# Attention and two feed-forward layers on one core: earlier norms, a shorter weight conversion, and engine order written out in the source

## The chip, the cores and the metric

The kernel runs on one core of a Trainium2 chip. Its time is the device time of one execution in microseconds (us); a smaller number is better. Five things run side by side and wait for each other by semaphores: TensorE (PE, matrix products into PSUM), VectorE (DVE), ScalarE (ACT), GpSimd (POOL), and the DMA engines, to which SyncE (SP) hands transfers. SBUF is the working memory.

## The reference

The input is q, k and v of 6016 rows (tokens) and 256 columns, all float32.

```python
qn = q / (np.linalg.norm(q, axis=1, keepdims=True) + 1e-06)   # columns scaled, over the 6016 rows
kn = k / (np.linalg.norm(k, axis=1, keepdims=True) + 1e-06)
s = kn.transpose(0, 2, 1) @ qn / tau                          # 256 x 256
a = np.exp(s - s.max(-1, keepdims=True)); a /= a.sum(-1, keepdims=True) + 1e-09
x = v @ a                                                     # 6016 x 256
h = x @ w_in                                                  # 256 -> 2048
P = a[0] + a[1] * h + a[2] * h**2 + a[3] * h**3
Q = 1.0 + np.abs(b[0]) * np.abs(h) + np.abs(b[1]) * h**2
y = (P / (Q + 1e-06)) @ w_out                                 # 2048 -> 256
h = y @ w_in2
out = (h * np.clip(h + 3.0, 0.0, 6.0) / 6.0) @ w_out2         # 6016 x 256
```

## The kernel before

**Opening: q and k.** q and k come in 14 chunks of up to 4 rows per partition (QK_CHUNKS, loop at line 173). Each chunk is multiplied into k^T q in PSUM (`sp`, line 196), squared on ACT (line 189) and added up on DVE (line 191) for the norms. Between chunks, four groups of the first input weights are loaded (`wi1`, W_IN_AT, line 177) and converted (`conv`). After the last chunk TensorE sums the squares over the partitions (line 215), DVE and ACT make the norms (lines 217 to 228), and a softmax of two halves follows (lines 232 to 249). Its transpose `eT` times `wi1` gives the fused weight `w1` (`emit_w1`, line 253), so that the first layer reads v directly.

**Weight conversion.** A float32 weight arrives as two words per number, and `conv` (line 102) rebuilds it as a float32 `f` from a low word L and a high word H: two ACT operations (lines 110 and 111), a DVE shift-and-or (line 112), and a second DVE operation for the sign bit (lines 116 and 119). Then `f` is split into a high part (ACT, line 123) and a rest (GpSimd, in two groups DVE, line 125). There are 16 groups: 4 each of `wi1`, `wo1`, `wi2`, `wo2`.

**The steps.** The 6016 tokens are one block of 384 and eleven of 512; each block has 8 steps for layer one, each step 256 of the 2048 columns. Step s runs, for different blocks at once: M1 (first product, line 281) into `h`; U1, U2, DS for the denominator, P1, P2, P3 for the numerator, LN and EX (the reciprocal as exp(-ln)); one step later HI, N2, DD, LO, which form the quotient as a high part and a rest; M3 (line 286), two steps later, into `y`. The second layer follows 10 steps behind: M2, C1, C2, H2, L2, and M4. Each of M1 to M4 is 12 matmuls. The end of a block adds Y (splitting y), O (the output) and V (splitting the next v). In steps below 20, DS is on GpSimd (line 338), below 16 LO too (line 459); L2 goes to GpSimd from step 17 on (line 393). `M1@4` below means M1 of step 4.

**What sets the order.** Each step is emitted by a list of names (ORDERS, one of three by step), with weight conversions at W; a scheduler then orders each engine's instructions by the time at which it expects them to be ready. Buffers are few (BUFS); `h` has two PSUM tiles in the first 10 steps and one afterwards. DMAs are issued by SP in the order of the source.

Of the kernel before, what the change touches and what calls it, by code (L numbers as in the profile page):

```python
# [41 lines left out]

@with_exitstack
def attention_rational_relu6_kernel(ctx: ExitStack, tc, q, k, vT, tau, w_in, w_out, ca, cb, w_in2, w_out2, outT):
# [128 lines left out]
    for i, n in enumerate(QK_CHUNKS):  # L173
# [3 lines left out]
        if i in W_IN_AT:  # L177
# [351 lines left out]
```

## Time and profile before

| | |
|---|---|
| median of 3 runs | 1174.41 us (1174.01 to 1175.34) |
| profiled execution | 1176.72 us, of which the span of the trace is 1175.0 us |
| busy share of the span | PE 95%, DVE 88%, ACT 70%, POOL 27% |
| mean granted TensorE clock | 0.976 of full speed |

The page divides the span into 40 slices and gives each engine's busy share in them. A busy PE is not a PE at its peak: at half its clock it is as busy as at the full one. So the granted clock stands beside the busy time, and the idle time of an engine counts only where it is the one that others wait for.

### The profile page before, as it was taken

Reading aid. Unit: us, or ns where it says so; the run is one execution under the profiler, and the core shown is the slowest. Engines: PE = TensorE matmul, PEld = TensorE weight load, DVE = VectorE, ACT = ScalarE, POOL = GpSimd, SP = SyncE. Lnnn points to the kernel's source line nnn. Section 1 sums busy time; section 2 is a strip of 40 time slices with the busy share of each in tenths; the row PEclk is TensorE's granted clock in tenths of the full one; section 3 lists DMA queues with packets and bytes.
Section 4 is the critical chain, followed back from the end, with each engine's and each line's share of the span. In section 5 each row is a group of like instructions: output and inputs, shape, how many; then the busy total and the mean of one; then the engine's idle time right before and its main releaser. Section 6 shows DMA issues by size and latency. Waiting matters only on the chain.

```text
span 1175.0 us, 12284 instructions
## 1 busy us (share of the span) xinstructions
PE 1110.8 (95%) x4858; PEld 915.3 (78%) x4858; DVE 1035.5 (88%) x861; ACT 822.3 (70%) x801; POOL 315.0 (27%) x136
## 2 busy tenths in 40 slices
PE   7866778899999999999999999999999999999998
PEld 6735666678888888888888888888888888888886
DVE  6699999999998998998998998998998998999943
ACT  6687786577767767777776776777777677776543
POOL 0027667633221222122122122222212212222200
PEclk9978989899999999999999999999999999999999
DMA  9952000001001001001001001001000000000000
GB/s 360 383 189 92 18 1 1 1 1 32 1 1 36 1 1 36 1 1 36 1 1 37 1 1 36 1 1 37 1 7 30 1 18 19 1 19 1 1 18 18
DMA packets 17450, 42.21 MB, mean 36 GB/s; under 512 B 1520, under 2 KB 2544, under 8 KB 17392
## 3 DMA queue, kind: packets, MB, share of 16 engines
q1 hardware_dynamic: 17392, 41.43, 9.7%
q8 instruction: 38, 0.62, 0.2%
q14 instruction: 20, 0.16, 0.0%
HBM read 35.26 MB, written 6.16 MB: 35 GB/s over the span
## 4 chain that ended last, share of the span: by engine, by line
PE 79%; DVE 6%; issue 4%; DMA 4%; POOL 3%; ACT 2%; SPq 1%; POOLq 0%; DVEq 0%; ACTq 0%
PE h L281 40%; PE o L286 20%; PE y L286 19%; DMA lo<-in_q_dram 2%; POOL B L338 1%; POOL lo L459 1%; DVE B L446 1%; DMA U<-in_k_dram 1%; DVE hi L440 1%; DVE P L452 1%; DMA raw_wo<-in_moe_w_out_dram 1%; DVE q L119 1%; DVE q L112 1%; DVE P L346 1%; DVE P L351 1%
## 5 line engine op out<-in xcount | busy, mean ns | idle before, releaser
L393 POOL TENSOR_TENSOR lo<-C,hi 128x1024 fp32r<-128x1024 f32 (+1 forms) x80 | 191.9, 2399 | 665.2 <-DVE lo L461 567.7
L281 PE MATMUL h<-vh,w 128*128 128x512 f32 (+1 forms) x768 | 193.5, 394 | 6.2 <-DVE P L351 6.0
L318 ACT ACTIVATE P<-h,col 128x1024 f32<-128x1024 f32 (+1 forms) x96 | 113.9, 1187 | 114.8 <-PE h L281 114.8
L286 PE MATMUL y<-hi,wo 128*128 128x512 f32 (+1 forms) x768 | 191.4, 391 | 2.3 <-DVE hi L440 2.3
L281 PE MATMUL h<-yh,wi 128*128 128x512 f32 (+1 forms) x768 | 187.8, 385 | 4.5 <-DVE C L383 3.9
L286 PE MATMUL o<-hi,wo 128*128 128x512 f32 (+1 forms) x768 | 186.8, 385 | 0.9 <-ACT hi L388 0.9
L281 PEld LDWEIGHTS h<-vh,w 128*128 128x128 f32 x768 | 146.7, 193 | 38.0 <-issue 8.5
L346 DVE TENSOR_TENSOR P<-P,h 128x1024 f32<-128x1024 f32 (+1 forms) x96 | 114.9, 1197 | 66.7 <-ACT U L326 61.7
L286 PEld LDWEIGHTS y<-hi,wo 128*128 128x128 f32 x768 | 146.0, 191 | 31.4 <-DVE hi L440 3.3
L281 PEld LDWEIGHTS h<-yh,wi 128*128 128x128 f32 x768 | 143.2, 188 | 33.9 <-DVE C L383 5.3
L286 PEld LDWEIGHTS o<-hi,wo 128*128 128x128 f32 x768 | 143.4, 188 | 29.1 <-ACT hi L388 1.3
L378 ACT ACTIVATE C<-h,imm 128x1024 f32<-128x1024 f32 (+1 forms) x96 | 105.6, 1100 | 66.1 <-PE h L281 66.1
L440 DVE SCALAR_TENSOR_TENSOR hi<-P,col,U 128x1024 fp32r<-128x1024 f32 (+1 forms) x96 | 134.4, 1400 | 3.2 <-ACT U L359 3.2
L446 DVE SCALAR_TENSOR_TENSOR B<-B,hi 128x1024 f32<-128x1024 f32 (+1 forms) x96 | 127.4, 1327 | 3.1
L383 DVE SCALAR_TENSOR_TENSOR C<-C,h 128x1024 f32<-128x1024 f32 (+1 forms) x96 | 114.5, 1193 | 17.3 <-ACT C L378 17.2
L286 PE MATMUL y<-lo,wo 128*128 128x512 f32 (+1 forms) x384 | 105.1, 397 | 25.3 <-POOL lo L459 24.8
L355 ACT ACTIVATE U<-B,imm 128x1024 f32<-128x1024 f32 (+1 forms) x96 | 108.9, 1134 | 27.1 <-POOL B L338 24.8
L452 DVE SCALAR_TENSOR_TENSOR P<-P,col,B 128x1024 f32<-128x1024 f32 (+1 forms) x96 | 122.8, 1279 | 2.9
L341 ACT ACTIVATE B<-B 128x1024 f32<-128x1024 f32 x76 | 80.7, 1062 | 62.2 <-DVE B L340 62.2
L351 DVE SCALAR_TENSOR_TENSOR P<-P,col,h 128x1024 f32<-128x1024 f32 (+1 forms) x96 | 120.3, 1253 | 0.1
L388 ACT ACTIVATE hi<-C 128x1024 fp32r<-128x1024 f32 (+1 forms) x96 | 98.7, 1028 | 14.3 <-DVE C L383 14.3
L286 PEld LDWEIGHTS y<-lo,wo 128*128 128x128 f32 x384 | 72.5, 192 | 43.3 <-POOL lo L459 29.0
(94 smaller groups left out, 1452.8 us busy)
## 6 DMA issues: line engine op xcount, KB each, us to landing
raw_wi<-in_moe_w_in_dram SPq DMA_DIRECT2D x8, 1024.0 KB, 11.0
raw_wo<-in_moe_w_out_dram SPq DMA_DIRECT2D x8, 1024.0 KB, 8.0
vo<-in_v_dram SPq DMA_DIRECT2D x11, 512.0 KB, 3.6
out_dram<-vo SPq DMA_DIRECT2D x11, 512.0 KB, 2.7
hi<-in_k_dram SPq DMA_DIRECT2D x5, 512.0 KB, 10.6
lo<-in_q_dram SPq DMA_DIRECT2D x5, 512.0 KB, 11.0
U<-in_k_dram SPq DMA_DIRECT2D x5, 512.0 KB, 12.7
P<-in_q_dram SPq DMA_DIRECT2D x5, 512.0 KB, 12.7
```

Source lines behind the costliest of these rows:

```text
L281: nc.tensor.matmul(h[:, j, 0:T], w_in_at(name, a, c, f + j), x[b][:, c, :], start=(i == 0), stop=(i == 5))
L286: nc.tensor.matmul(y[:, d, 0:T], w_out_at(name, a, 2 * pr + j, d), g[b][:, j, :], start=(pr == 0 and i == 0), stop=(pr == 7 and i == 5))
L318: nc.scalar.activation(out=halves(c["P"], T), in_=c["h"], func=AF.Identity, scale=A3, bias=A2)
L346: nc.vector.tensor_tensor(out=p, in0=p, in1=c["h"], op=ALU.mult)
L351: nc.vector.scalar_tensor_tensor(out=p, in0=p, scalar=A1, in1=c["h"], op0=ALU.add, op1=ALU.mult)
L355: nc.scalar.activation(out=c["U"][:, f], in_=c["B"][:, f], func=AF.Ln, bias=C_ONE)
L378: nc.scalar.activation(out=halves(c["C"], T2), in_=c["h2"], func=AF.Relu, bias=C_THREE)
L383: nc.vector.scalar_tensor_tensor(out=cv, in0=cv, scalar=6.0, in1=c["h2"], op0=ALU.min, op1=ALU.mult)
L393: i2 = e.tensor_tensor(out=c["L2"][:, f2], in0=c["C"][:, f2], in1=c["H2"][:, f2].bitcast(F32), op=ALU.subtract)
L440: nc.vector.scalar_tensor_tensor(out=c["Hi"][:, fa], in0=P[:, fa], scalar=A0, in1=U[:, fa], op0=ALU.add, op1=ALU.mult)
L446: nc.vector.scalar_tensor_tensor(out=B[:, fa], in0=B[:, fa], scalar=ONE_EPS, in1=c["Hi"][:, fa].bitcast(F32), op0=ALU.add, op1=ALU.mult)
L452: c["last"] = nc.vector.scalar_tensor_tensor(out=P[:, fa], in0=P[:, fa], scalar=A0, in1=B[:, fa], op0=ALU.add, op1=ALU.subtract)
```

## The change

The loads change place: only `wi1` group 0 is loaded among the q and k chunks (at chunk 8), groups 1 to 3 after the last chunk; the constants come at chunk 4, and the `wi2` loads right after `wo1`. The squares of k and q get a buffer kind each, and TensorE sums the squares, now folded to 256 columns by DVE, before the last three chunks' products: chunk 11, the norm broadcast, then chunks 12 and 13. The k norm's scaling is no longer a separate ACT operation, and the copy of `eT` is made by DVE. In the conversion, one ACT operation (a parametric relu with slope -2^32) puts the sign bit in place while scaling, so the second DVE operation goes.

DS is on DVE in every step (with an Abs on ACT behind it, now called AB), and U2 goes. LO runs on GpSimd (LOP) or on DVE by the written list, L2 likewise. FILL is a written list of everything from the first `w1` product to step 18; after it each step runs ORDER. `chain` ties every instruction of PE, DVE, ACT and GpSimd to the one before it in the source, so the scheduler no longer moves any. `shares` and `behind` make a GpSimd weight rest or L2 start only after the last DVE operation that was marked before it in the source.

```diff
-W_IN_AT = [2, 4, 6, 8]
-CONV_AT = [6, 8, 10, 12]
-CONST_AT = 9
+W_IN_AT = [8, 13, 13, 13]
+CONST_AT = 4
+NORM_AT = 10
-POOL_LO, POOL_D = 16, 20
...
+ORDER = "M1 U1 P1 Vh M2 DS P2 P3 C1 AB LN Vl M3 C2 Yh Yl EX H2 M4 HI N2 DD LO L2P O"
+FILL = (
+    "wo1:2s W0a wo1:1s wo1:0j E0ah0 W0b E0ah1 wo1:2b E0al0 E0al1 E0bh0 M1@0 wo1:2j E0bh1 wo1:0h E0bl1 E0bl0 wo1:1b wo1:0l W1 "
...
+    def chain(start):
+
+        last = {}
+        for i in nc.cur_bb.bb.instructions[start:]:
+            if i.engine in ORDERED:
+                if i.engine in last:
+                    tc.add_manual_dep(i, last[i.engine].name, mybir.DependencyInfo(
+                        mybir.DependencyClass.NoSync, mybir.DependencyReason.DATA), reason="program order")
+                last[i.engine] = i
...
-        nc.scalar.activation(out=f, in_=H.bitcast(F32), func=AF.Copy, scale=2.0 ** -112)
-        nc.scalar.activation(out=L, in_=L16, func=AF.Identity, scale=2.0 ** -13, bias=C_LOW)
-        nc.vector.scalar_tensor_tensor(out=q, in0=q, scalar=3, in1=L, op0=ALU.logical_shift_left, op1=ALU.bitwise_or)
...
-        nc.vector.scalar_tensor_tensor(out=q, in0=H, scalar=-0x80000000, in1=q, op0=ALU.bitwise_and, op1=ALU.bitwise_or)
...
+        if part == "s":
+            nc.scalar.activation(out=c["q"].bitcast(F32), in_=c["H"].bitcast(F32), func=AF.Prelu, scale=2.0 ** -112, alpha=-2.0 ** 32)
+        elif part == "b":
+            nc.scalar.activation(out=c["L"], in_=c["L16"], func=AF.Identity, scale=2.0 ** -13, bias=C_LOW)
+        elif part == "j":
...
+            shares(nc.vector.scalar_tensor_tensor(out=f, in0=c["q"], scalar=3, in1=c["L"],
+                                                  op0=ALU.logical_shift_left, op1=ALU.bitwise_or))
...
+        elif part == "h":
+            nc.scalar.activation(out=w[:, 0:1024], in_=c["f"], func=AF.Copy)
+        else:
+            e = nc.vector if part == "l" else nc.gpsimd
...
+    products(NORM_AT + 1)
...
+    nc.tensor.matmul(ssp[:, 1, 0:256], ones, diag, start=True, stop=True)
+    for i in range(NORM_AT + 2, LAST + 1):
+        products(i)
...
-                    nc.scalar.activation(out=c["B"][:, f], in_=c["U"][:, f], func=AF.Identity, scale=aB1, bias=aB0)
...
-                    nc.gpsimd.tensor_tensor(out=B[:, f], in0=B[:, f], in1=c["U"][:, f], op=ALU.mult)
...
+                nc.vector.scalar_tensor_tensor(out=halves(c["B"], T), in0=halves(c["U"], T), scalar=aB0, in1=c["h"], op0=ALU.add, op1=ALU.mult)
```

In FILL, `wo1:2s` is part s of converting group 2 of `wo1` (s and b on ACT, j on DVE, h on ACT, then l for the rest on DVE or p on GpSimd); `W0a` is the product for half of `w1` group 0, and `E0ah0`, `E0al0` its copies out of PSUM (high part on ACT, rest on DVE).

TensorE's instructions at the end of q and k, before (`y` is k^T q, `o` the sums of squares and then the norm broadcast, `h` the transpose and then `w1`):

```order
L196 MATMUL y<-lo,hi 128x256 x6
L196 MATMUL y<-P,U 128x256 x2
L215 MATMUL o<-ones,accs 128x1 x2
L215 MATMUL o<-ones,B 128x1
...
L229 MATMUL o<-P,ones 128x256
L246 MATMUL h_390<-ident,P 128x128 x2
L257 MATMUL h_416<-raw_wi_115,hi 128x512
```

The same place now:

```order
L285 MATMUL o<-ones,accs 128x1
L286 MATMUL o<-ones,st 128x1
L250 MATMUL y<-P,U 128x256 x8
L307 MATMUL o<-yl,ones 128x256
L250 MATMUL y<-lo,hi 128x256 x6
L250 MATMUL y<-P,U 128x256 x2
L329 MATMUL h_406<-ident,yl 128x128 x4
L345 MATMUL o<-raw_wi_233,hi 128x256 x4
```

The products of the last three chunks have moved behind the sums of squares, and the broadcast stands between them.

DVE in the first block, before (HI writes `hi`, N2 writes `B`, DD is `P<-P,col,B`, P2 and P3 read `h` in PSUM):

```order
L440 SCALAR_TENSOR_TENSOR hi<-P,col,U 128x768
L346 TENSOR_TENSOR P<-P,h_655 128x768
L446 SCALAR_TENSOR_TENSOR B<-B,hi 128x768
L351 SCALAR_TENSOR_TENSOR P<-P,col,h_655 128x768
L452 SCALAR_TENSOR_TENSOR P<-P,col,B 128x768
```

The same place now:

```order
L523 SCALAR_TENSOR_TENSOR hi<-P,col,U 128x768
L431 SCALAR_TENSOR_TENSOR P<-P,col,h_608 128x768
L529 SCALAR_TENSOR_TENSOR B<-B,hi 128x768
L535 SCALAR_TENSOR_TENSOR P<-P,col,B 128x768
L417 TENSOR_TENSOR P<-P,h_634 128x768
L422 SCALAR_TENSOR_TENSOR B<-U,aB_362,h_634 128x768
```

DS (line 422) has come onto DVE, and behind DD, which frees GpSimd's LO, now stand operations that read `h`.

GpSimd from its first operation on tiles of a step, before (`wo` and `wi` are weight rests, `B` is DS, `lo<-P,U` is LO):

```order
L125 TENSOR_TENSOR wo_598<-q,wo_598 128x1024
L338 TENSOR_TENSOR B<-B,U 128x768 x2
L459 TENSOR_TENSOR lo<-P,U 128x768
L338 TENSOR_TENSOR B<-B,U 128x768
L125 TENSOR_TENSOR wi_835<-q,wi_835 128x1024
```

The same place now:

```order
L171 TENSOR_TENSOR wo_483<-q,wo_483 128x1024
L540 TENSOR_TENSOR lo<-P,U 128x768
L171 TENSOR_TENSOR wo_564<-q,wo_564 128x1024
L540 TENSOR_TENSOR lo<-P,U 128x768 x6
L171 TENSOR_TENSOR wo_961<-q,wo_961 128x1024
```

The DS operations have left GpSimd, and six LOs follow one another without a weight between them.

## Rows read from the trace of the kernel before

**Rows 1.** Page, part 2: busy tenths in 40 equal slices.

```profile
PE   7866778899999999999999999999999999999998
```

**Rows 2.** Windows: stretch; length, busy us (instructions) by engine; PEclk, DMA share, GB/s.

```profile
74.50:279.40 204.90, 166.43 (x714) 136.03 (x713) 193.33 (x147) 148.15 (x159) 118.79 (x45) 0.92 0.11 38
279.40:1169.00 889.60, 888.71 (x3921) 735.58 (x3920) 789.07 (x654) 623.75 (x584) 187.66 (x78) 1.00 0.03 11
```

**Rows 3.** Timeline of TensorE: start, busy us, what [idle before, releaser].

```profile
9.89 3.71 PE L196 MATMUL y<-lo,hi 128*128 128x256 f32 x16 [0.28 <-DMA lo<-in_q_dram]
...
44.92 3.62 PE L196 MATMUL y<-lo,hi 128*128 128x256 f32 x16
...
55.28 0.50 PE L215 MATMUL o<-ones,accs 128*128 128x1 f32 x4
...
63.52 1.22 PE L229 MATMUL o<-P,ones 128*128 128x256 f32 x2 [5.36 <-DVE P L227]
...
78.57 0.62 PE L281 MATMUL h<-vh,w 128*128 128x384 f32 x2
...
279.43 1.98 PE L281 MATMUL h<-vh,w 128*128 128x512 f32 x8
```

**Rows 4.** Waits of TensorE, 74.5 to 279.4 us: total, times, longest.

```profile
PE y L286 <- POOL lo L459: 24.8, 10, 7.0
```

**Rows 5.** Timeline of DVE, 600 to 635 us.

```profile
611.00 1.22 DVE L346 TENSOR_TENSOR P<-P,h 128x1024 f32<-128x1024 f32 x1
612.13 1.28 DVE L340 SCALAR_TENSOR_TENSOR B<-U,aB,h 128x1024 f32<-128x1024 f32 x1
...
621.88 1.22 DVE L346 TENSOR_TENSOR P<-P,h 128x1024 f32<-128x1024 f32 x1 [1.11 <-ACT U L326]
```

**Rows 6.** Windows, a stretch in the loading of q and k.

```profile
20.00:24.00 4.00, 3.40 (x16) 2.72 (x15) 3.18 (x4) 4.00 (x4) 0.00 (x0) 1.00 1.03 410
```

**Rows 7.** Timeline of DVE, 49 to 75 us.

```profile
50.96 0.69 DVE L186 TENSOR_TENSOR accs<-accs 128x512 f32<-128x512 f32 x1
...
58.20 0.16 DVE L217 TENSOR_SCALAR small<-o 128x4 f32<-128x4 f32 x1 [5.68 <-PE o L215]
...
67.97 0.74 DVE L241 TENSOR_TENSOR P<-P,o 128x256 f32<-128x256 f32 x2
...
74.57 1.23 DVE L112 SCALAR_TENSOR_TENSOR q<-q,raw_wo 128x1024 int32<-128x1024 int32 x1 [0.32 <-ACT raw_wo L111]
```

**Rows 8.** DVE by line and shape, 74.5 to 279.4 us: busy, mean ns, idle before.

```profile
L440 DVE SCALAR_TENSOR_TENSOR hi<-P,col,U 128x1024 fp32r<-128x1024 f32 x11 | 22.5, 2044 | 0.0
L446 DVE SCALAR_TENSOR_TENSOR B<-B,hi 128x768 f32<-128x768 f32 x8 | 14.5, 1813 | 0.1
L351 DVE SCALAR_TENSOR_TENSOR P<-P,col,h 128x768 f32<-128x768 f32 x8 | 8.1, 1007 | 0.1
L383 DVE SCALAR_TENSOR_TENSOR C<-C,h 128x768 f32<-128x768 f32 x8 | 7.5, 944 | 0.0
L264 DVE SCALAR_TENSOR_TENSOR w<-h,small,w 128x512 fp32r<-128x512 f32 x4 | 3.0, 746 | 0.0
```

**Rows 9.** DVE by line and shape, 400 to 1100 us.

```profile
L440 DVE SCALAR_TENSOR_TENSOR hi<-P,col,U 128x1024 fp32r<-128x1024 f32 x64 | 81.9, 1280 | 0.0
L461 DVE TENSOR_TENSOR lo<-P,U 128x1024 fp32r<-128x1024 f32 x65 | 79.5, 1224 | 2.0
```

**Rows 10.** Timeline of GpSimd and DVE, 226 to 240 us.

```profile
227.70 3.21 POOL L459 TENSOR_TENSOR lo<-P,U 128x1024 fp32r<-128x1024 f32 x1 [3.32 <-DVE P L452]
...
236.48 2.40 POOL L125 TENSOR_TENSOR wo<-q,wo 128x1024 fp32r<-128x1024 f32 x1 [2.25 <-ACT wo L123]
...
228.59 3.40 DVE L440 SCALAR_TENSOR_TENSOR hi<-P,col,U 128x1024 fp32r<-128x1024 f32 x1
```

**Rows 11.** ACT: the table load (timeline), and line 110 by shape, 0 to 78 us.

```profile
0.73 1.28 ACT L51 ACT_TABLE_LOAD   x1 [0.73 <-PEq L513]
...
L110 ACT ACTIVATE q<-raw_wi 128x1024 f32<-128x1024 f32 x5 | 5.8, 1153 | 5.4 <-DMA raw_wi<-in_moe_w_in_dram 5.4
```

More of the change, by code (lines that the diff above doesn't have):

```diff
@@ L163, in attention_rational_relu6_kernel, with fold, load_chunk, squares @@
     acc_q, acc_k = accs[:, 0:1024], accs[:, 1024:2048]
+    start = len(nc.cur_bb.bb.instructions)
     nc.gpsimd.memset(accs, 0.0)
+    warm = ptile("h2")
+    for _ in range(6):
+        nc.tensor.matmul(warm[:, 0, 0:128], ones, ones, start=True, stop=True)
     sp = ptile("y")
     ssp = ptile("o")
[L167 to L170 removed]
     LAST = len(QK_CHUNKS) - 1
[L172 to L173 removed]
+    first = [sum(QK_CHUNKS[:i]) for i in range(LAST + 1)]
+    chunks, tails = [], []
+    def fold(a, n):
+        nc.vector.tensor_tensor(out=a[:, 0:n], in0=a[:, 0:n], in1=a[:, n:2 * n], op=ALU.add)
+    def load_chunk(i):
+        n = QK_CHUNKS[i]
         kt, qt = (wtile(QK_TAGS[j][i % 2])[:, 0:n * 256] for j in range(2))
         for t, src in ((kt, kv), (qt, qv)):
[L176 to L177 removed]
+            nc.sync.dma_start(out=t.rearrange("p (r c) -> p r c", r=n), in_=src[:, first[i]:first[i] + n, :])
+        chunks.append((kt, qt))
+    def squares(i):
+        n = QK_CHUNKS[i]
+        for t, a in zip(chunks[i], (acc_k, acc_q)):
+            s2 = wtile("B" if t is chunks[i][0] else "st")[:, 0:n * 256]
+            nc.scalar.activation(out=s2, in_=t, func=AF.Square)
+            if i < LAST:
+                nc.vector.tensor_tensor(out=a[:, 0:n * 256], in0=a[:, 0:n * 256], in1=s2, op=ALU.add)
+            else:
+                tails.append(s2)
+    def products(i):
+        kt, qt = chunks[i]
+        for r in range(QK_CHUNKS[i]):
+            for c in range(2):
+                nc.tensor.matmul(sp[:, c, 0:256], kt[:, r * 256 + c * 128:r * 256 + (c + 1) * 128],
+                                 qt[:, r * 256:(r + 1) * 256], start=(first[i] + r == 0), stop=(first[i] + r == PER - 1))
+    n_wi = 0
+    for i in range(LAST + 1):
+        load_chunk(i)
+        for _ in range(W_IN_AT.count(i)):
             load_w("wi1", n_wi)
@@ L468, in step @@
-        assert not ops, ops.keys()
-    aB0 = const.tile([128, 1], F32, name="aB0")
-    aB1 = const.tile([128, 1], F32, name="aB1")
-    nc.scalar.activation(out=aB0, in_=B0, func=AF.Abs)
-    nc.scalar.activation(out=aB1, in_=B1, func=AF.Abs)
-    def need(name, g, late=False):
-        if (name, g) in done:
-            return
-        done.add((name, g))
-        if name == "w1":
-            need("wi1", g)
-            emit_w1(g)
-        else:
-            if name == "wi2" and g == 0:
-                for i in range(4):
-                    load_w("wi2", i)
-                    load_w("wo2", i)
-            conv(name, g, late)
@@ new lines, in lo, with do @@
+                if e is nc.vector:
+                    shares(i)
+            ops["LO"] = lambda: lo(nc.vector)
+            ops["LOP"] = lambda: lo(nc.gpsimd)
+        return ops
+    steps = {}
+    def do(n, at):
+        if at not in steps:
+            steps[at] = instructions(at)
+        if n in steps[at]:
+            steps[at].pop(n)()
+            for same in (("LO", "LOP"), ("L2", "L2P")):
+                if n in same:
+                    for x in same:
+                        steps[at].pop(x, None)
```

376 lines of the change are left out of this document (188 added, 188 removed), and 22 rows, old and new, of tables (FILL, ORDERS).

## The prediction

> **What bounds the kernel now.** I read the busy tenths first. TensorE stays under nine tenths in the first eight slices of 29.4 us and is full afterwards [rows 1]. So the loss lies in the first 240 us. The windows say the same more sharply: from 279.4 to 1169 us TensorE is busy for 888.7 of 889.6 us at a granted clock of 1.00 [rows 2]. The reader is to see that nothing can be gained there except by less TensorE work, and the change takes none away. 279.43 us is where M1 of step 20 starts [rows 3]. The question is therefore how much earlier that matmul starts, and whether the stage behind it stays gap-free.
>
> Between 74.5 and 279.4 us DVE is busy for 193.3 of 204.9 us, ACT for 148.2, GpSimd for 118.8, TensorE for 166.4 [rows 2]. TensorE's longest sum of waits in that stretch is 24.8 us for LO on GpSimd [rows 4], but LO needs DD, which is DVE's. So DVE, 94% busy, is the bound of the opening steps, and its idle 11.6 us are all that is left there. Ahead of that lies a chain: the last q and k products end at 55.28 us, and M1 of step 0 starts at 78.57 [rows 3], 23.3 us later.
>
> **Part 1: the repeating stage.** The strict order replaces the scheduler's there. A step has the same eight large DVE operations as before, with DS ahead of P2, and DVE now sits idle for 1.11 us in a step until U1 is done [rows 5]. U1 is now ACT's first operation after M1, so DS can start when U1 ends, and P1 runs beside DS. The third DVE operation still frees `h` for the next M1. L2 stays on GpSimd behind LO. I cost this part at 0. Its cover is the 1.11 us per step; if that went and 0.4 us more, TensorE would wait in every step (a rival below).
>
> **Part 2: an earlier start.** Three loads of 1.05 MB no longer stand among the chunks. At 410 GB/s [rows 6] they took 2.56 us each, 7.7 us together. The q and k chunks, 1.05 MB each, then arrive every 2.56 us, while TensorE needs 3.62 us for each operand pair of 16 passes [rows 3], so TensorE sets the pace: nine chunks from 9.89 us end at 42.5. The last fold of squares on DVE ended at 50.96 + 0.69 = 51.65 us [rows 7]; less 7.7 and plus two more folds of about 0.4 (an estimate from the 0.69 of twice the width) makes 44.7. That is 2.2 us in which TensorE waits, the price of putting the sums ahead. The sums took 12 pairs from 55.28 to 58.20 us [rows 3, 7]; eight pairs take 1.9, to 46.6. Chunk 11 covers the norms until 50.2. The chain from the sums to the broadcast took 58.20 to 63.52, 5.3 us [rows 3, 7], with weight conversions in between on both engines; they now stand behind it, so I take 4.0, and the broadcast starts at 50.6. It lasts 1.22 us [rows 3], chunks 12 and 13 another 3.5, to 55.3. From the first score operation (67.97) to the DVE merge of the last `wo1` group (74.57) went 6.6 us [rows 7], more than half of it conversions; I take 3.2 without them. DVE's first merge behind the softmax then starts at 58.5 us instead of 74.57, **16.1 us earlier**. Bounds: 11.4 (the 5.3 and the 6.6 us kept whole) and 17.7 (the chain wholly under chunk 11, and 2.0 us for the softmax).
>
> The loads that moved behind the last chunk are 3 of `wi1`, then v and `wo1`: in the order of SP, `wi1` group 3 lands 7.7 us after the last chunk and the first `wo1` 3.5 us later, ahead of their conversions. No queue of GpSimd carries a DMA.
>
> **Part 3: DVE's own work up to M1 of step 20.** Prices: 1.28 us for an operation with a column scalar on 1024 elements, 1.22 for the others [rows 9]; 1.007 and 0.944 on 768, 0.746 on 512 [rows 8]; a third to half of that on 256, say 0.4. Before, in the 74.5 to 279.4 us stretch, 147 instructions: 33 x 1.28 + 50 x 1.224 + 24 x 1.007 + 32 x 0.944 + 8 x 0.746 = 163.8. One instruction starts up to 0.09 us before the end shown for the one ahead of it [rows 5], on the mean 0.07 I estimate, which takes off 10.3: 153.5 us of own work.
>
> After, from the first merge to P3 of step 19, by the new order: 44 x 1.28 (DS 12, P3 12, HI 10, DD 10) + 49 x 1.224 (P2 12, N2 10, LO 6, merges 12, weight rests 5, and 4 more) + 32 x 1.007 + 33 x 0.944 + 6 x 0.746 + 4 x 0.4 = 185.6, less 168 x 0.07, is 173.8 us. The 18 conversion operations of before become 12, but 20 DS, 3 weight rests and 3 LOs come. So DVE's own work grows by **20.3 us**. This speaks against the change.
>
> **Part 4: what DVE loses to GpSimd.** 193.3 less 153.5 is 39.8 us that DVE was busy beyond its own work. The rows show where: HI took 2044 ns on the mean instead of 1280, N2 on 768 elements 1813 instead of 944 [rows 8, 9], while P3, which reads `h` in PSUM, stayed at 1007. One case: HI started at 228.59 us beside an LO on GpSimd that ended at 230.91, and ended 1.08 us after it, at 231.99 [rows 10]. It waited and then ran. The LO was itself 0.8 us longer than the 2.40 of a free GpSimd operation of that width [rows 10]. So the two engines exclude each other when DVE reads two SBUF tensors, and reading PSUM is free of it. Before, 45 GpSimd instructions stood in the stretch [rows 2]: 0.88 us of loss each. After, by the order, 20: seven weight rests, eleven LOs, two L2s. At the same rate that is 17.6 us. At the other end it is 0, if DVE reads PSUM whenever GpSimd runs: behind DD, which frees LO, the list mostly puts two or three of DS, P2, P3, together 1.9 to 3.7 us. Between 0 and 17.6 I take 6, since most, not all, are placed so: **33.8 us less lost**.
>
> The Trainium skill, SBUF — State Buffer, section "Who interferes with whom", has it as a lock: whichever of the two starts first keeps the shared ports for its whole instruction and the other is fully blocked. The trace agrees (1.08 us after GpSimd's end). By that rule what matters is not how many instructions there are but which start first, and a badly timed LO would cost DVE the whole of it; that is the second rival's case.
>
> **Part 5: the rest.** ACT gets 20 Abs for 20 U2, about the same length, and a parametric relu in place of a scaled copy of 1.15 us [rows 11]. Its cost is not in the trace; between 0.4 us less and 1.3 more each (a table load, [rows 11]) I take the same 1.15. With 148 us of work in a stretch of 190, ACT hides that. TensorE's six added products of ones run while it waits for the first chunk.
>
> **Sum.** Start -16.1; DVE own work +20.3; lock -33.8; DVE idle unchanged at 11.6, between 4 (little room to wait in a denser list) and 22 (an engine in strict order waits where the scheduler took something else). Together -29.6 us: M1 of step 20 starts near 250 us. The profiled execution took 1176.7 (span 1175.0 plus 1.7), so it would take 1147.1; the median shown is 2.3 us lower, so I forecast 1145.
>
> **Rivals.** *More is gained.* The lock vanishes (-6), idle falls to 5 (-7), the start comes 18 us earlier (-2): 1130. For it: TensorE's and ACT's busy sums leave 25 us of room below DVE's. Against: strict order pays for every duration that differs from plan. Chance 0.13.
>
> *The lock stays and the order waits.* The LOs and rests start at bad moments, 17.6 us lost (+12), and DVE waits 22 us (+10): 1167. For it: only the weight rests and L2 are tied behind DVE's marked operations; an LO starts as soon as DD ends, and a late P2 puts HI beside it. Against: DD's successors read PSUM. Chance 0.18, of which 0.03 ends within 0.2% of no change.
>
> *Slower: the repeating stage opens gaps.* From step 20 to 95 all four products run, 76 steps. If DVE in fixed order (C2 behind P3, HI behind C2) overran a step by 0.5 us, TensorE would wait each time: +38 against -30, 1153 to 1183 as the loss per step goes from 0.1 to 0.5, and slower from about 0.4 us. For it: the strict list lets a late C1 hold back HI, N2, DD and LO behind it. Against: 1.11 us of slack in each step [rows 5]. Chance of reaching that point 0.07.
>
> *The conversion doesn't become shorter*, because the relu makes ACT reload its function table: 32 loads of 1.28 us [rows 11] are 41 us, ACT's work rises to 189, 9 above DVE's 180, and with 5 us more ahead of the first step the gain falls to about 15: 1160. For it there is nothing in rows; the new order has one load, as before. Chance 0.02. The Trainium skill, ScalarE: Activation LUTs, section "Table sets: the hidden batching unit", states that functions come in sets and that a switch costs a load. One load for ln, exp, copy and abs agrees with it; no run here shows the relu.
>
> **How the numbers follow.** The forecast case, 1135 to 1157, has 0.60. Faster: 0.60 + 0.13 + 0.15 + 0.02 = 0.90. Same: 0.03. Slower: 0.07. About 0.2%, 2.3 us, is what a measurement of this kernel can tell from no change. The range 1126 to 1167 takes in the first rival and the near part of the second; it leaves out 0.07 on the slow side, the far half of the second rival and a little below.
>
> **What would show it.** M1 of step 0 near 61 us and of step 20 near 250. P2, P3 and DS at their prices, HI and N2 close to 1.28 and 1.22 in the opening, and DVE busy for about 180 us in it. TensorE without gaps from step 20 on at clock 1.00. Part 2 is wrong if the sums of squares wait beyond 47 us; part 4 if HI and N2 stay near 2 us; part 1 if TensorE waits for DVE after 300 us. A start of step 20 later than 277 us would make the whole forecast wrong.

## The result and the profile after

The changed kernel takes 1154.24 us (median of 4 runs, 1153.15 to 1155.82) against 1174.76 us: a ratio of 0.9827 with a 95% interval of 0.981 to 0.9844. The forecast was 1145 us, the range 1126 to 1167. The time lies in the range and the kernel is faster, as forecast, but 9 us of the forecast gain did not come.

The windows of the profiled execution (span 1152.3 us), to be laid beside [rows 2]:

```profile
63.90:256.70 192.80, 163.86 (x725) 136.92 (x723) 176.28 (x170) 154.60 (x167) 44.34 (x20) 0.93 0.13 42
256.70:1146.50 889.80, 888.91 (x3920) 735.97 (x3921) 796.56 (x655) 621.94 (x583) 187.90 (x78) 1.00 0.03 11
```

The second line is the same stage as in the kernel before, of the same length and as full. So the whole gain is made ahead of M1 of step 20, which starts at 256.69 us instead of 279.43 [rows 3]: 22.7 us, the difference of the spans. (Between the medians it is 20.5 us: the profiled execution of the kernel before took 2.3 us more than its median, that of the changed kernel, 1154.25, did not.) It has three parts. DVE's first merge of a `wo1` weight stands at 63.91 us instead of 74.57 [rows 7]: 10.7. From there DVE is busy 17.0 us less (176.28 instead of 193.33). And it is idle for 16.5 us instead of 11.6, which takes 4.9 back.

TensorE's timeline shows the start and the way into the repeating stage (answers to [rows 3]):

```profile
10.28 3.69 PE L250 MATMUL y<-lo,hi 128*128 128x256 f32 x16 [2.04 <-DMA lo<-in_q_dram]
...
37.99 3.62 PE L250 MATMUL y<-lo,hi 128*128 128x256 f32 x16
46.94 0.56 PE L285 MATMUL o<-ones,accs 128*128 128x1 f32 x2 [5.34 <-DVE accs L227]
...
50.35 5.74 PE L250 MATMUL y<-P,U 128*128 128x256 f32 x16
55.93 0.59 PE L307 MATMUL o<-yl,ones 128*128 128x256 f32 x2
...
66.81 1.76 PE L375 MATMUL h<-vh,w 128*128 128x384 f32 x8
...
246.21 3.40 PE L375 MATMUL h<-vh,w 128*128 128x512 f32 x8 [3.44 <-DVE P L431]
...
256.69 2.08 PE L375 MATMUL h<-vh,w 128*128 128x512 f32 x8 [0.71 <-DVE P L431]
```

TensorE waits 5.34 us for the folded squares, and then chunk 11 takes 5.74 us where a chunk of the same 16 passes took 3.62. The windows show what goes with it: the granted clock, 1.00 from 40 to 41.6 us, falls while TensorE waits.

```profile
41.60:46.90 5.30, 0.00 (x1) 0.00 (x0) 5.30 (x8) 4.07 (x8) 0.00 (x0) 0.75 1.02 403
46.90:50.30 3.40, 3.36 (x16) 3.39 (x17) 1.53 (x3) 0.64 (x1) 0.00 (x0) 0.50 1.05 388
50.30:56.00 5.70, 5.70 (x18) 4.71 (x19) 3.38 (x11) 4.70 (x6) 0.00 (x0) 0.63 1.05 386
```

The last column but two is the clock: 0.50 (1.2 GHz) in the sums of squares, and 0.63 in chunk 11, a mean of the lower and the full level. The same pair, a wait of 3.44 us and then eight matmuls in 3.40 us instead of 2.08, stands at 246.21.

DVE in the start and at the end of the opening (answers to [rows 7] and [rows 5]):

```profile
40.02 1.23 DVE L160 SCALAR_TENSOR_TENSOR raw_wi<-q,raw_wi 128x1024 int32<-128x1024 int32 x1 [0.94 <-ACT raw_wi L156]
...
45.17 1.96 DVE L227 TENSOR_TENSOR accs<-accs 128x512 f32<-128x512 f32 x4
...
52.30 0.48 DVE L304 TENSOR_SCALAR yl<-ident,small 128x128 f32<-128x128 f32 x2
...
60.01 0.48 DVE L325 SCALAR_TENSOR_TENSOR yl<-y,small,yh 128x256 f32<-128x256 f32 x1 [1.35 <-PE y L250]
...
63.91 1.21 DVE L160 SCALAR_TENSOR_TENSOR q<-q,raw_wo 128x1024 int32<-128x1024 int32 x1
...
242.46 1.22 DVE L417 TENSOR_TENSOR P<-P,h 128x1024 f32<-128x1024 f32 x1 [1.97 <-ACT U L412]
...
252.82 1.28 DVE L422 SCALAR_TENSOR_TENSOR B<-U,aB,h 128x1024 f32<-128x1024 f32 x1 [4.29 <-ACT P L407]
...
621.00 1.28 DVE L422 SCALAR_TENSOR_TENSOR B<-U,aB,h 128x1024 f32<-128x1024 f32 x1 [0.98 <-ACT P L407]
```

At 40.02 a weight conversion stands ahead of the last squares and folds. At 52.30 the norms are ready for the broadcast, which TensorE reaches only behind chunk 11, at 55.93. And DS (L422), which reads U1's result, waits for P1, in the repeating stage too.

DVE by line and shape, 64 to 256 us (answers to [rows 8]): HI, N2 and P3, with mean ns behind the busy time.

```profile
L523 DVE SCALAR_TENSOR_TENSOR hi<-P,col,U 128x1024 fp32r<-128x1024 f32 x10 | 12.9, 1292 | 0.3 <-ACT U L439 0.2
...
L529 DVE SCALAR_TENSOR_TENSOR B<-B,hi 128x768 f32<-128x768 f32 x8 | 7.6, 952 | 0.0
...
L431 DVE SCALAR_TENSOR_TENSOR P<-P,col,h 128x768 f32<-128x768 f32 x8 | 8.1, 1008 | 0.0
```

HI has gone from 2044 to 1292 ns and N2 from 1813 to 952. Summed over all groups of the opening (number of operations times mean, less the undisturbed price of that operation from [rows 8, 9]), the time above the prices is 1.2 us.

### The profile page after: what moved, and what is told of

It is laid out like the page before. It is cut to its first block, busy times and chain, and to the rows that moved or that the text cites. A ratio compares the mean times of both kernels' runs of the same rounds, so it can differ in the third digit from the quotient of the medians.

```text
span 1152.3 us, 12288 instructions
## 1 busy us (share of the span) xinstructions
PE 1106.5 (96%) x4870; PEld 918.3 (80%) x4870; DVE 1013.2 (88%) x876; ACT 819.1 (71%) x799; POOL 234.9 (20%) x109
## 4 chain that ended last, share of the span: by engine, by line
PE 84%; DVE 9%; DMA 3%; ACT 3%; issue 1%; SPq 0%; DVEq 0%; ACTq 0%
PE h L375 42%; PE o L380 21%; PE y L380 19%; DMA lo<-in_q_dram 2%; DVE B L422 1%; DVE P L417 1%; DVE B L529 1%; DVE P L431 1%; DVE hi L523 1%; DVE P L535 1%; PE y L250 1%; DMA U<-in_k_dram 1%; ACT U L412 1%; ACT P L407 1%; PE o L345 0%
## 5 line engine op out<-in xcount | busy, mean ns | idle before, releaser
L412 ACT ACTIVATE U<-h,col 128x1024 f32<-128x1024 f32 (+1 forms) x96 | 105.7, 1101 | 188.6 <-PE h L375 187.5
L375 PE MATMUL h<-vh,w 128*128 128x512 f32 (+1 forms) x768 | 196.3, 399 | 19.1 <-DVE P L431 12.1
L380 PE MATMUL y<-hi,wo 128*128 128x512 f32 (+1 forms) x768 | 186.9, 385 | 0.0
L422 DVE SCALAR_TENSOR_TENSOR B<-U,aB,h 128x1024 f32<-128x1024 f32 (+1 forms) x96 | 120.7, 1257 | 63.0 <-ACT P L407 60.0
L523 DVE SCALAR_TENSOR_TENSOR hi<-P,col,U 128x1024 fp32r<-128x1024 f32 (+1 forms) x96 | 122.1, 1272 | 0.3 <-ACT U L439 0.2
L529 DVE SCALAR_TENSOR_TENSOR B<-B,hi 128x1024 f32<-128x1024 f32 (+1 forms) x96 | 116.0, 1208 | 2.8
L540 DVE TENSOR_TENSOR lo<-P,U 128x1024 fp32r<-128x1024 f32 (+1 forms) x85 | 103.8, 1221 | 2.8
## 6 DMA issues: line engine op xcount, KB each, us to landing
raw_wo<-in_moe_w_out_dram SPq DMA_DIRECT2D x8, 1024.0 KB, 10.1
```

What stands on the lines that cost most here:

```text
L375: nc.tensor.matmul(h[:, j, 0:T], w_in_at(name, a, c, f + j), x[b][:, c, :], start=(i == 0), stop=(i == 5))
L380: nc.tensor.matmul(y[:, d, 0:T], w_out_at(name, a, 2 * pr + j, d), g[b][:, j, :], start=(pr == 0 and i == 0), stop=(pr == 7 and i == 5))
L412: nc.scalar.activation(out=halves(c["U"], T), in_=c["h"], func=AF.Abs, scale=B1)
L422: nc.vector.scalar_tensor_tensor(out=halves(c["B"], T), in0=halves(c["U"], T), scalar=aB0, in1=c["h"], op0=ALU.add, op1=ALU.mult)
L523: shares(nc.vector.scalar_tensor_tensor(out=c["Hi"][:, fa], in0=P[:, fa], scalar=A0, in1=U[:, fa], op0=ALU.add, op1=ALU.mult))
L529: shares(nc.vector.scalar_tensor_tensor(out=B[:, fa], in0=B[:, fa], scalar=ONE_EPS, in1=c["Hi"][:, fa].bitcast(F32), op0=ALU.add, op1=ALU. ...
```

## The experiments

Every time is a median, with its ratio to the kernel before and the 95% interval of that ratio in brackets; the changed kernel's is 1154.2 (0.981 to 0.9844). Starts are read from one profiled execution of each version. "M1@20" is the start of M1 of step 20 (256.69 in the changed kernel), "M1@0" that of step 0 (66.81), "first merge" that of DVE's first shift-and-or on a `wo1` weight (63.91), and the "score operation" is the first of the softmax on DVE (60.01).

**e1: norms behind all products.**

```diff
-        if i <= NORM_AT:
-            products(i)
+        products(i)
...
-    products(NORM_AT + 1)
...
-    for i in range(NORM_AT + 2, LAST + 1):
-        products(i)
```

> The norms are no longer beside the last rows: all products of k and q first, then the sums of squares, the norms, the broadcast. Marks of the changed kernel: sums of squares start at 46.94 us, first score operation 60.01, M1 of step 0 at 66.81, M1 of step 20 at 256.69, span 1152.3. Theory A (the wait of 5.3 us ahead of the sums, and the slow clock behind it, cost more than the norms' place beside chunk 11 hides): TensorE runs chunks 11 to 13 without a gap until 48.6 (3.45 + 2.65 + 0.9 us), the sums take 1.9 us at full clock, the chain to the broadcast 2.2, and the score operation comes at about 57.5, set by the conversions on ACT; M1 of step 0 near 64.3, M1 of step 20 near 254, span near 1150, that is 2 to 3 us FASTER than the changed kernel. Theory B (the place beside chunk 11 is where the earlier start comes from): the 4 us of the chain come back, M1 of step 0 at 69 to 71, span 1155 to 1157.

Measured: 1155.6 us (0.9832, 0.9817 to 0.9847); sums from 50.63 us, first merge 63.57, M1@0 68.14, M1@20 258.39. Neither size came. In the profiled execution chunk 2 ran at the slow clock, 5.38 us instead of 3.69, and all products ended 2 us later than expected, which blurs theory A. The step that theory B forecast did not come either: M1@0 lies 1.3 us behind that of the changed kernel, not 2 to 4, and the medians 1.4, with intervals that overlap. So no gain of the norms' place, as the change has it, is clear of the noise.

**e2: the sign on DVE again.**

```diff
-            nc.scalar.activation(out=c["q"].bitcast(F32), in_=c["H"].bitcast(F32), func=AF.Prelu, scale=2.0 ** -112, alpha=-2.0 ** 32)
+            nc.scalar.activation(out=c["q"].bitcast(F32), in_=c["H"].bitcast(F32), func=AF.Copy, scale=2.0 ** -112)
...
+            shares(nc.vector.scalar_tensor_tensor(out=f, in0=c["H"], scalar=-0x80000000, in1=c["q"],
+                                                   op0=ALU.bitwise_and, op1=ALU.bitwise_or))
```

> The parametric relu becomes a scaled copy again, and a second DVE operation puts the sign in, 16 times: 4 ahead of the first step, 12 between it and step 20. Theory A (the opening is bound by DVE's own work): the 12 cost 12 x (1.22 - 0.07) = 13.8 us between the first merge of a wo1 weight and M1 of step 20 (192.8 us becomes 205 to 208), and the one ahead of the folds another 1.2; span 1166 to 1169. ACT's relu and copy are the same length (1.14 us), so no gain on ACT. Rival C (the opening is bound by the written order and by waits between engines; DVE's 16.5 idle us take the added work in): the stretch grows by 0 to 6 us, span 1152 to 1160.

Measured: 1164.8 us (0.9913, 0.9895 to 0.9931); first merge to M1@20 202.65 us instead of 192.78. The group that came, on weights of the steps:

```profile
L162 DVE SCALAR_TENSOR_TENSOR q<-raw_wo,q 128x1024 int32<-128x1024 int32 x8 | 9.8, 1226 | 0.3
```

DVE's busy time between the two marks grew by 14.1 us and its idle time fell by 4.3, so 9.9 came through: between the two theories, nearer to A. Without the relu 10.6 of the 20.5 us between the medians are lost. (The weights are 64-bit floats, which is why each has a high and a low word: a group of 256 by 512 is 1.05 MB.)

**e3: conversion behind the squares.**

```diff
-        if i == W_IN_AT[0] + 3:
-            for p in "sbj":
-                conv("wi1", 0, p)
         squares(i)
+        if i == LAST:
+            for p in "sbj":
+                conv("wi1", 0, p)
```

> The conversion of wi1 group 0 (2.3 us on ACT, 1.2 us on DVE) moves from in front of the squares of chunk 11 to behind those of the last chunk. Theory A (the conversion is what makes the folds late): squares, adds and folds end 2.2 us earlier, the sums start at 44.6 to 44.8 instead of 46.94 as first forecast, TensorE waits 3.1 us instead of 5.3, M1 of step 0 near 64.6, span near 1150. Rival D (the last chunks' arrival sets the folds): sums stay at 46.5 to 47 us and the span at 1152.

Measured: 1151.4 us (0.9801, 0.9782 to 0.9821); M1@0 65.86, M1@20 256.83. TensorE:

```profile
46.29 0.35 PE L285 MATMUL o<-ones,accs 128*128 128x1 f32 x2 [2.79 <-DVE accs L227]
...
48.08 5.37 PE L250 MATMUL y<-P,U 128*128 128x256 f32 x16
```

The sums came only 0.65 us earlier, but here chunk 9 had landed 1.27 us later (its square on ACT at 34.19 instead of 32.92). If that delay is added, the conversion costs 1.9 us, and once it is gone the chunks' arrival sets the folds (ACT then waits for data ahead of its squares). Both theories hold a part. Chunk 11 ran slow again, behind a wait of only 2.79 us; the sums between them were still at full clock. The profiled execution was the slowest of the four (1154.35), and the interval of the median overlaps that of the changed kernel, so a gain in time is not shown.

**e4: one more chunk ahead of the sums.**

```diff
-NORM_AT = 10
+NORM_AT = 11
```

> NORM_AT 11 instead of 10: chunk 11 (16 pairs) is multiplied ahead of the sums, in the time in which TensorE waited, and chunk 12 covers the norms, chunk 13 comes behind the broadcast. Theory A (wait and slow clock of TensorE ahead of the sums are lost time): TensorE waits 1.9 us instead of 5.3 (41.45 + 3.45 to 46.94), the granted clock stays above 0.9, the eight sum pairs take about 2 us instead of 3.4, the last products end near 53; the score operation then waits for the conversions on ACT and DVE, at about 56.3 instead of 60.0. M1 of step 0 near 63, span near 1148.5. Rival (chunk 11 was a good cover and chunk 12 with 2.7 us is too short; the clock falls anyway): score operation 59 to 60, span 1151 to 1152.

Measured: 1152.0 us (0.9805, 0.9786 to 0.9823). TensorE did not wait ahead of the sums, and kept its clock from there up to the softmax:

```profile
10.52 5.38 PE L250 MATMUL y<-lo,hi 128*128 128x256 f32 x16 [2.82 <-DMA lo<-in_q_dram]
...
48.52 2.84 PE L250 MATMUL y<-lo,hi 128*128 128x256 f32 x12
...
59.34 3.55 PE L345 MATMUL o<-raw_wi,hi 128*128 128x256 f32 x8 [0.52 <-DVE hi L331]
```

The score operation came at 55.66 (56.3 expected) and the first merge at 59.81, 4.1 us earlier. M1@0 gained only 2.5, since the first `w1` product, behind a wait of 4.73 us, took 3.55 instead of 1.99. M1@20 came at 254.41, 2.3 earlier. These marks are theory A's; the time is not clear of the noise (the interval overlaps the changed kernel's, and 1150.0 us of span lie between the two forecasts). And one mark is luck: the wait of 1.9 us that was expected ahead of the sums is missing because chunk 2 had run at the slow clock (first line), so that TensorE came to the sums 1.7 us later.

**e5: order left to the scheduler.**

```diff
-    chain(start)
```

> The written order is only proposed: the ties from each instruction to the one before it on its engine go, so the scheduler places TensorE, DVE, ACT and GpSimd again by its own times; all operations are those of the changed kernel (sign by relu, norms before the last rows in the source, DS on DVE, LO by the list). Theory A (the gain is mostly in the operations: shorter conversion, fewer GpSimd operations that DVE stands beside): span within 5 us of the changed kernel's 1152, TensorE still without gaps after 300 us. Rival F (the written order itself carries the gain: it keeps two-SBUF operations of DVE away from GpSimd and the queues fed): the opening grows by 10 to 25 us, HI and N2 rise from 1.28 to 1.6 us and more, span 1162 to 1177.

Measured: 1170.7 us (0.9959, 0.9944 to 0.9973), span 1168.6. TensorE is full after 300 us here as well (700.0 of 700 us from 400 to 1100), and the first merge came 3 us earlier, at 60.90. So 19.3 us were lost behind the first merge, 17.0 of them up to M1@20 (270.65). The window between the two marks, and LO on DVE, which reads two SBUF tensors:

```profile
60.90:270.65 209.75, 175.18 (x756) 143.43 (x756) 193.91 (x175) 160.08 (x171) 50.56 (x21) 0.94 0.13 45
...
L540 DVE TENSOR_TENSOR lo<-P,U 128x1024 fp32r<-128x1024 f32 x6 | 10.7, 1783 | 0.0
```

LO's price is 1.22 us; with the other groups 11.3 us stand above the prices, instead of 1.2. DVE is busy 17.6 us more than in the changed kernel and idle 0.7 less. So the 17.0 us are DVE's own time: 10.1 beside GpSimd, and most of the rest five more operations ahead of M1@20 (175 instead of 170). That is rival F in its times: without the written order 16.4 of the 20.5 us go. Its sign came only in part: LO rose to 1.78 us, but N2 to 1.42 and HI stayed at 1.29, where 1.6 and more were forecast for both. The losses of e2, e5 and e6 add up to more than the gain, so they are not shares of it.

**e6: loads among the chunks.**

```diff
-W_IN_AT = [8, 13, 13, 13]
+W_IN_AT = [2, 4, 6, 8]
...
-        if i == W_IN_AT[0] + 3:
+        if i == 11:
```

> The four wi1 loads stand among the chunks again (at chunks 2, 4, 6, 8), as before the change; their conversions stay where the changed kernel has them. Three loads of 1.05 MB at about 410 GB/s are 2.56 us each. Theory A (the squares follow the arrival of the chunks, so the loads count in full): the sums start 5.5 to 7.7 us later than at 46.94, TensorE waits for chunks between 10 and 42 us, M1 of step 0 at 72 to 74, span 1157 to 1160. Rival G (TensorE's 3.45 us for a chunk pair sets the pace and hides them, and the loads behind the last chunk come that much earlier): sums within 2 us, span 1152 to 1154.

Measured: 1162.9 us (0.9892, 0.9877 to 0.9907). TensorE:

```profile
54.17 0.56 PE L285 MATMUL o<-ones,accs 128*128 128x1 f32 x2 [4.19 <-DVE accs L227]
```

The sums came 7.2 us later, the first merge 7.8 (71.67) and M1@20 8.2 (264.86). This is theory A, with M1@0 (74.57) and the span (1160.5) half a microsecond beyond its ranges: the chunks' arrival sets the squares, and three loads are 7.7 us.

**e7: GpSimd not held behind DVE.**

```diff
     def behind(i):
-        if port[0] is not None:
+        if False:
```

> The weight rests and L2 on GpSimd no longer wait for the DVE operation marked ahead of them; they start when their data are there. Nothing else changes. Theory A (GpSimd beside a DVE operation on two SBUF tensors costs DVE the time, and the ties keep them apart): in the opening the seven rests and two L2 cost about 0.9 us each as before the change, span 3 to 8 us longer, seen as HI, N2 or LO well over 1.28 us; in the repeating stage L2 costs DVE up to 1.1 us per step, which its idle time takes in, TensorE stays without gaps. Rival H (order on each engine already places them; the ties only make GpSimd wait): opening the same within 1.5 us, span 1151 to 1153.

Measured: 1264.6 us (1.0752, 1.0734 to 1.077). The opening is the same (M1@20 258.84, first merge 65.59). The loss came where both theories had none. GpSimd and DVE in one step of the repeating stage:

```profile
616.69 2.40 POOL L471 TENSOR_TENSOR lo<-C,hi 128x1024 fp32r<-128x1024 f32 x1 [9.61 <-ACT hi L467]
...
616.75 3.42 DVE L529 SCALAR_TENSOR_TENSOR B<-B,hi 128x1024 f32<-128x1024 f32 x1
```

L2 now starts when H2 is done, 0.06 us ahead of N2, and N2 ends 1.08 us after L2, as in [rows 10]. N2 takes 2.2 us more, DVE has 0.98 to give, and a step lasts 12.01 us instead of 10.88. In 76 steps that is 86 us; DVE's 19 splits of v and y, which its slack had hidden, add about 1.14 us each, 22. Together 108; from M1@20 to the end it took 108.8 more. The Trainium skill, SBUF — State Buffer, section "Who interferes with whom", says that the order of issue decides who blocks; the trace agrees: 0.06 us of it cost 2.2.

**e8: five rests to GpSimd.** In the written list, here and for `wo1:3`, `wi2:0`, `wo2:0` and `wo2:3`:

```diff
-wo1:0l
+wo1:0p
...
```

> The five weight rests that the written list gives to DVE (wo1 groups 0 and 3, wi2 group 0, wo2 groups 0 and 3) go to GpSimd, behind the marked DVE operation. Theory A (the opening is bound by DVE's own work, GpSimd has 148 of 193 us free): DVE's work falls by 5 x 1.15 = 5.8 us, 12 operations more having given 9.9 us for 13.8 of work, so the opening gets 3 to 4.5 us shorter, less what GpSimd takes from DVE at 0.1 to 0.9 us each: span 1148 to 1151. Rival J (a rest of 2.4 us on GpSimd comes later than one of 1.22 us on DVE and M3 or M4 waits for it, and it blocks DVE): span 1153 to 1158.

Measured: 1153.3 us (0.9808, 0.979 to 0.9827); M1@20 258.03. DD beside them:

```profile
L535 DVE SCALAR_TENSOR_TENSOR P<-P,col,B 128x1024 f32<-128x1024 f32 x10 | 16.3, 1628 | 0.0
```

DVE was spared 5 x 1.15 = 5.8 us and lost 6.9 more beside GpSimd (8.1 above the prices instead of 1.2), and the stretch from the first merge (63.09) to M1@20 got 2.2 us longer. The medians are 0.9 us apart with intervals that overlap: no gain, where theory A had 3 to 6 us. At 1.4 us for each of the five, a GpSimd operation that DVE has to stand beside cost DVE more here than doing the work.

**e9: DS ahead of P1 in the source.**

```diff
-ORDER = "M1 U1 P1 Vh M2 DS P2 P3 C1 AB LN Vl M3 C2 Yh Yl EX H2 M4 HI N2 DD LO L2P O"
+ORDER = "M1 U1 DS P1 Vh M2 P2 P3 C1 AB LN Vl M3 C2 Yh Yl EX H2 M4 HI N2 DD LO L2P O"
```

> In the source DS stands ahead of P1 (in every step from 19 on, and in steps 0, 2, 4, 16, 17), and P2 of step 18 ahead of U1; the order on every engine stays the same. In the changed kernel DS, which reads U1's result, starts only when P1 ends, 0.98 us later, and P2 of step 18 only when U1 ends, though it reads P1's (idle of DVE 1.97 us at 242.46 and 4.29 us at 252.82). Theory A (the wait is one semaphore count, set by what stands ahead in the source): DS starts when U1 ends, P2 of step 18 about 1.1 us earlier, M1 of step 19 with it, DS of step 19 another 1.0, so M1 of step 20 comes 2 to 3 us earlier than 192.8 us behind the first wo1 merge, span near 1149.5; in the repeating stage DVE's idle time moves but TensorE stays full, no gain there. Rival K (DS waits for P1 for another reason, a shared read of h): P1 then waits for DS or nothing changes, stretch 192 to 196 us, span 1152 or more.

Measured: 1208.3 us (1.0278, 1.0258 to 1.0298). DVE, ACT, DVE in one step:

```profile
617.05 1.27 DVE L422 SCALAR_TENSOR_TENSOR B<-U,aB,h 128x1024 f32<-128x1024 f32 x1
...
618.36 1.21 ACT L407 ACTIVATE P<-h,col 128x1024 f32<-128x1024 f32 x1 [4.62 <-DVE B L422]
...
619.59 1.22 DVE L417 TENSOR_TENSOR P<-P,h 128x1024 f32<-128x1024 f32 x1 [1.27 <-ACT P L407]
```

Rival K: two reads of `h` by different engines run one after the other, in the order of the source. P1 now waits for DS and P2 for P1, 1.27 us of idle DVE per step instead of 0.98. The trace of the kernel before had shown it already. ACT there runs P1 (L318), then U1 (L326):

```profile
619.63 1.21 ACT L318 ACTIVATE P<-h,col 128x1024 f32<-128x1024 f32 x1 [0.98 <-PE h L281]
620.74 1.10 ACT L326 ACTIVATE U<-h,col 128x1024 f32<-128x1024 f32 x1
```

P2, which reads P1's result and `h` but not U1's, starts at 621.88 [rows 5], when U1 ends, and not at 620.84, when P1 ends. Neither theory had the size: the stretch to M1@20 took 199.6 us, and the loss in the repeating stage was in none. From M1@20 on it took 48.3 us more. A step lasts 11.17 us instead of 10.88, which in 76 steps is 21 to 22; the steps with a split of v last 12.30 and those with a split of y 12.77, which adds 9 x 1.13 + 10 x 1.60 = 26. The Trainium skill, PSUM — Partial Sum Buffer, section "PSUM bank collisions raise a hardware error", has the rule: a compiler's scheduler adds a dependency between any two instructions on different engines that touch the same bank, reads included. The trace agrees as to the wait; what sets the dependency in this kernel no run shows.

**e10 and e11: the start rearranged as well; M4 ahead of M1.** Both still hold the edit of e9. e11 has e10's start and names `M4@19` ahead of M1 of step 19 in the written list.

```diff
-NORM_AT = 10
+NORM_AT = 11
...
+    for p in "sb":
+        conv("wi1", 2, p)
     nc.scalar.activation(out=ln, in_=ss, func=AF.Ln)
...
-    split_v(0, "l")
-    for p in "sb":
-        conv("wo1", 0, p)
...
     nc.vector.reciprocal(out=rs, in_=rs)
+    for p in "sb":
+        conv("wo1", 0, p)
+    conv("wi1", 3, "j")
+    split_v(0, "l")
```

> The previous change, and in the start: NORM_AT 11; the conversion of wi1 group 2 on ACT ahead of the norms' logarithm (where ACT stood idle for 2.1 us), DVE's merge of group 3, the split of v and the conversion of wo1 group 0 behind the softmax, where DVE and ACT stood idle for 2.8 us. Theory A (the start is one chain, and what DVE and ACT do between its links counts only where they are not idle): the score operation comes at about 53 us, as soon as the last products end (52.65), instead of 60.0 (55.66 with NORM_AT 11 alone); M1 of step 0 near 61, M1 of step 20 near 248 to 250, span 1143 to 1146. Rival L (the work put behind the softmax delays the first steps as much as the chain gains, ACT being full from 57 to 91 us): M1 of step 0 at 62 to 64, span 1147 to 1149.

> The previous kernel, and M4 of step 19 ahead of M1 of step 19 on TensorE, where it waited 3.4 us and M1 then ran 3.4 us instead of 2.08 for its first eight. Theory A (the slow clock behind the wait is on the path M1, U1, DS, P2, P3, next M1): M1 of step 19 at full clock, M1 of step 20 1.3 us earlier than in the previous kernel; but TensorE then waits about 3 us ahead of M1 of step 20, and that one may run slow: span 0 to 1.3 us shorter. Rival M (TensorE's idle sum is the same, only at another place): same within 0.3 us or slower by up to 1.5.

Measured: e10 1205.5 us (1.0249, 1.023 to 1.0268), M1@20 259.05, 6.0 earlier than in e9; e11 1202.6 (1.0225, 1.0207 to 1.0244), M1@20 258.61, though its first merge came 1.1 later. M1 of step 19 was at full clock in e11 (2.08), but M1@20 then ran slow (2.83). In e10 TensorE waited only 1.10 us ahead of the sums, and yet chunk 12 took

```profile
49.01 4.19 PE L250 MATMUL y<-lo,hi 128*128 128x256 f32 x12
```

instead of 2.84 in e4. That kept the score operation at 54.93 instead of 53, and M1@0 at 64.62, beyond both forecasts. In e11, with the same start and a wait of 1.07 us, chunk 12 took 5.47:

```profile
48.74 5.47 PE L250 MATMUL y<-lo,hi 128*128 128x256 f32 x12
```

For M4's place, theory A's signs came, the slow M1@20 among them. The stretch from the first merge to M1@20 got 1.5 us shorter, but the intervals of e10 and e11 overlap.

**e12: the best start, with TensorE kept busy.** Without the edit of e9; e10's start, M4 of step 19 ahead of M1, and eleven products of ones:

```diff
     s2k, s2q = tails
+    for _ in range(5):
+        nc.tensor.matmul(warm[:, 0, 0:128], ones, ones, start=True, stop=True)
...
+    for _ in range(6):
+        nc.tensor.matmul(warm[:, 0, 0:128], ones, ones, start=True, stop=True)
     nmax, sm, rs = small[:, 28:30], small[:, 30:32], small[:, 2:4]
```

> The changed kernel with the order DS had there (U1, P1, DS), with the new start of the run before last (NORM_AT 11, conversions moved off the norms' chain), M4 of step 19 ahead of M1 of step 19, and eleven products of ones on TensorE whose result nobody reads: five ahead of the sums, six ahead of the transposes, where it waited 1.1 and 1.8 us and then ran slow. Theory A (the start is one chain; waits of TensorE cost twice, once as a wait and once as slow clock behind it; the repeating stage is left alone): chunk 12 in 2.7 us instead of 4.2 to 5.5, the first w1 products in 2 + 1.9 us instead of 3.8 + 2.8, first wo1 merge near 59.5, M1 of step 0 near 61, M1 of step 20 near 250, TensorE without gaps from there, span 1144 to 1147, median 1146 to 1149. Rival N (the work moved behind the softmax costs the first steps as much; the products of ones come in the way): M1 of step 20 at 253 to 256, span 1149 to 1152.

Measured: 1150.2 us (0.9786, 0.9773 to 0.9799), span 1146.7. TensorE:

```profile
9.91 5.38 PE L250 MATMUL y<-lo,hi 128*128 128x256 f32 x16 [2.22 <-DMA lo<-in_q_dram]
...
49.03 2.84 PE L250 MATMUL y<-lo,hi 128*128 128x256 f32 x12
...
56.69 1.99 PE L351 MATMUL o<-raw_wi,hi 128*128 128x256 f32 x8 [0.52 <-DVE hi L333]
58.52 1.89 PE L351 MATMUL h<-raw_wi,hi 128*128 128x256 f32 x8
...
249.45 3.42 PE L381 MATMUL h<-vh,w 128*128 128x512 f32 x8 [3.44 <-DVE P L437]
```

Theory A: full clock from the sums to M1@0 (chunk 2, the first line, ran slow), first merge 59.15, M1@0 60.70, M1@20 249.45, 7.2 us earlier than in the changed kernel. M1@20 itself ran slow, and its step lasts 12.62 us instead of 10.99, which gives 1.6 back. The span is in theory A's range, the median 1.2 us above it. The interval does not touch that of the changed kernel: this version beats both. Up to M1@0 it differs from e10 by the products of ones and, in this execution, by the slow chunk 2; in e10 chunk 12 took 4.19 us and the first `w1` products 3.78 and 2.78, in e12 they took 2.84, 1.99 and 1.89. How much of the 4.0 us between e12 and the changed kernel is theirs, and how much the other moves', no run separates.

## Why the prediction was right, and where it was not

The frame held. The repeating stage kept its length, so part 1 was rightly put at 0; the gain was to be M1@20's, and it was. M1@20 was forecast at 250 and came at 256.7, M1@0 at 61 and came at 66.8. Of the 9 us that are missing, 6.9 are M1@20's: part 2 gave 5.4 us too little, part 3 cost 1.3 more, DVE's idle time 4.9 more, and part 4 gave 4.8 more. That part 4's surplus covers most of part 2's shortfall is luck. The other 2.3 us come from the last line of the sum, which took the 2.3 us between profiled execution and median over to the changed kernel, where they did not occur.

**Part 2 failed in its size: 10.7 us instead of 16.1, outside its own bounds.** Five terms: the sums began at 46.94 instead of 44.7 (+2.2), took 3.4 us instead of 1.9 (+1.5), chunk 11 covered the norms until 55.9, 5.6 us instead of 4.0 (+1.6), broadcast and chunks 12 and 13 took 4.1 instead of 4.7 (-0.6), the softmax 3.9 instead of 3.2 (+0.7). The first is the `wi1` conversion (about 1.9 us, e3), which the changed source puts ahead of the squares of chunk 11 and the sum left out, and the chunks' arrival (e3, e6). The second and third go back to one step: the prediction let TensorE wait 2.2 us and priced what came behind at full clock. The wait was 5.34 us, since the sums came late and since chunks follow each other by 3.46 us (37.99 less 10.28, by eight), not by the 3.62 that each is shown busy, so that the ninth ended at 41.6 and not 42.5. Behind it the clock was at 0.50 and 0.63. The chain of the norms, priced at 4.0, took only 2.4 (50.35 to 52.8); it was slow chunk 11 that held the broadcast. e4 and e12 had no such wait, and their sums and chunk 12 ran at full clock; in the nine traces with a wait of 1.07 us or more ahead of the sums (the changed kernel, e2, e3 and e6 to e11), the chunk behind them ran slow. The part's first term, 7.7 us for the loads, was right (e6: 7.8). Its own sign of being wrong, sums beyond 47 us, did not show: they came at 46.94.

**Part 3 was right.** DVE's own work in the opening is 176.3 less 1.2, 175.1 us, against 173.8; the work that it counts against the change is there (e2 shows the price of adding to it).

**Part 4 was right in its mechanism and took too much for the rest:** 1.2 us are lost beside GpSimd where 6 were taken. What it missed is where the guard matters. In the opening the ties that hold GpSimd behind DVE concern nine operations, and nothing is lost there without them; in the repeating stage their lack costs 109 us (e7). The opening is guarded by the order (e5: 11.3 us lost beside GpSimd without it, though the ties stayed).

**Part 5 was right.** The relu takes 1.13 us against 1.15 for the copy, and the trace has one table load as before, so that rival is out.

**DVE's idle time, taken as unchanged at 11.6, came out at 16.5.** Part 1's sentence that DS starts when U1 ends and P1 runs beside it was wrong: DS waits for P1 (621.00, e9), and [rows 5] held the same wait the other way round. In the repeating stage that costs nothing; in the opening it is 1.0 to 1.1 us in each of the waits of 1.97 and 4.29 us at 242.46 and 252.82. The rest of the added idle time was not traced. The rival of slower steps did not come, but little kept it away: e7 and e9 reach its outcome, at 1.13 and 0.28 us per step and the splits on top, by causes that it did not name, and each is slower than the kernel before.

## What to carry to other kernels

Price what stands behind a wait of TensorE at the slow clock until a row shows otherwise. Fill such a wait with work that is due anyway, as e4 does with chunk 11, or, where there is none, with products that nobody reads, as e12 does. A guard that keeps GpSimd off a nearly full DVE has to be judged at the stage that repeats, not where it is written. When two engines read one PSUM tile, look in the trace whether the second waits for the first, as here in the kernel before, in the changed one and in e9: then the order of the source is an order in time.
